# VectorE in source order from the first attention tile on, and ScalarE's part of a weight chunk one step sooner

## The chip, the core and the metric

The kernel runs on one core of a Trainium2 chip. A core has five engines with queues of their own: TensorE (matrix products, PE in the profile), VectorE (DVE), ScalarE (ACT), GpSimd (POOL) and SyncE (SP, which here only issues DMAs). They run side by side and wait for each other through semaphores; inside one queue everything happens in the order in which it stands there. The metric is the device time of one execution in microseconds (us).

## The reference

Attention with a position bias, and a gated feed-forward block behind it, all in float32:

```python
scores = scale * q @ k.T + bias            # q, k, v: 4 batches x 8 heads x 576 x 64
bias   = relu(x @ w1 + b1) @ w2            # x = log1p(|i-j|) / log1p(max(i,1)); hidden 32
attn   = softmax(scores) @ v               # -> x: 2304 tokens x 512
out    = ((x @ w_a) * (x @ w_b)) @ w_out   # w_a, w_b: 512 x 1536; w_out: 1536 x 512
```

The weights come as 64-bit numbers and are turned into 32-bit floats on the core.

## The kernel before

**Attention tiles.** The work is cut into 144 tiles of 128 query rows by 576 keys. A unit is a pair of heads of a batch; units 0 to 15 (tiles 0 to 63) are the first 256 rows of all batches, the others the rest. The first 16 tiles take their scores two at a time (`qk_pair`), from then on `qk` fills one buffer, which the next tile needs empty. For one tile: `qk` on TensorE; `soft1` (L539: the softmax pass on VectorE, which adds the bias, scales and takes the row minimum `mn`; L544: the exponential on ScalarE, with the row sum `sm`); `soft2` (L589: GpSimd adds a small number to the sum; L590: VectorE's reciprocal; L595: GpSimd multiplies the tile by it); `turn` (L607: five transposes on TensorE, copied back by ScalarE); and per unit `pv` (L635), whose output is split into two halves of 16 bits by ScalarE (L648) and VectorE (L650, the remainder). From unit 12 on `split_turn` (L574, L577, a DMA transpose) takes the place of the multiplication and `turn`. `prep_k`, `prep_q` and `prep_v` split K, Q and V of the units from 8 on the same way: ScalarE makes the upper half (L419, L433, L460), VectorE the remainder (L416, L435, L461).

**Weights.** 24 chunks of w_a and w_b, then 12 of w_out. A chunk is loaded (`w_load`), and `w_unit` turns it: ScalarE multiplies the upper word (L266), VectorE shifts it (L268), puts in three bits of the lower word (L269) and the sign (L272). For w_a and w_b a step `s` of `wab_steps` holds the conversion of chunk s, ScalarE's maximum over chunk s-1 (L289), every fourth step a power-of-two scale that goes through TensorE twice (`pow2_down`, L79 to L87, and `pow2_up`, L92, L94), and the split of chunk s-7 (`wab_parts`: L306 GpSimd, L309 ScalarE, L310 GpSimd). The tile `wt` that a chunk fills comes from two rings of four and is free again after L310, so chunk s needs the tile of chunk s-8. For w_out the split is L313 and L314 in the same step.

**MoE.** `moe_main` runs in blocks of 256 tokens: per 128 of the 1536 columns two half-steps of 12 matmuls (L768), ScalarE's scaled copy `asb` (L776) and VectorE's product `g` (L752, the gate); then `moe_out` (L812).

**What sets the order.** `merge` lays the generators side by side in source order: attention half-steps (`asteps`, two per tile), MoE half-steps (`main`) and weight steps (`wts`). Weight steps lie between tiles 0 and 46; the first MoE block begins at tile 19. TensorE issues in source order throughout (`manual_schedule`). VectorE does so only from the middle of the second MoE block on, which is tile 46 (`SOON`); ahead of it, and for ScalarE, GpSimd and SyncE throughout, a planner with a timing model picks the order. Around `SOON` the order in the source changes: below it a tile's `soft1` stands in its first half-step and `soft2` of the tile before at the end; from it on `soft2(n)` is followed by `soft1(n+1)`, and the remainders of K, Q and V (`lows`) are put off until after that.

## Time and profile before

| | us |
|---|---|
| median of 3 runs (lowest to highest) | 756.22 (755.72 to 757.78) |
| the profiled execution | 754.13 |
| its span, first to last instruction | 752.3 |
| TensorE busy | 699.4 (93%) |
| VectorE busy | 497.0 (66%) |
| ScalarE busy | 449.1 (60%) |
| GpSimd busy | 333.1 (44%) |
| mean granted TensorE clock | 0.984 |

The profiled execution is one run; its own time is a little under the median of the three. The busy shares are means over stages with different loads. A matmul's end is modelled, so a busy TensorE need not be at its peak.

### The profile page before, as it was taken

The numbers are of one execution on the slowest core, as the hardware profiler recorded it, in microseconds if no ns is written. First come the engines' busy times: TensorE is split into PE (matmuls) and PEld (weight loads), VectorE is DVE, ScalarE is ACT, GpSimd is POOL, SyncE is SP. The second block draws the span as 40 slices with busy tenths as digits, with TensorE's granted clock in tenths as the row PEclk, the third lists the DMA queues.
The fourth block names the chain that finished last, engine by engine and source line by source line (L and its number), as shares of the span: only waits on it lengthen the run. The fifth ranks groups of instructions, "written<-read, shape, count | busy, mean of one in ns | idle before, by whom it ended". The sixth has DMA issues, their size and how long they took to land.

```text
span 752.3 us, 15601 instructions
## 1 busy us (share of the span) xinstructions
PE 699.4 (93%) x5451; PEld 533.1 (71%) x5451; DVE 497.0 (66%) x1204; ACT 449.1 (60%) x1005; POOL 333.1 (44%) x477
## 2 busy tenths in 40 slices
PE   7787898899899999998899989999999999999997
PEld 2255465577787556676787768878888887888886
DVE  7768688858984576766798888888987781111100
ACT  6868887877876678754555556656655562321310
POOL 3437668865863123332354445634553562311200
PEclk9979999999999999999999999999999999999999
DMA  8998776477754887799999999999999974000001
GB/s 247 322 370 279 241 224 212 147 256 251 248 149 119 219 200 195 187 201 204 246 251 253 225 274 244 248 228 276 246 236 271 222 142 130 1 1 29 2 15 42
DMA packets 178163, 147.69 MB, mean 196 GB/s; under 512 B 125092, under 2 KB 138148, under 8 KB 178084
## 3 DMA queue, kind: packets, MB, share of 16 engines
q1 hardware_dynamic: 170928, 130.92, 69.4%
q10 hardware_dynamic: 5876, 10.93, 5.3%
q0 software_dynamic: 1280, 4.84, 1.8%
q8 instruction: 43, 0.70, 0.4%
q14 instruction: 36, 0.29, 0.1%
HBM read 101.15 MB, written 17.18 MB: 157 GB/s over the span
## 4 chain that ended last, share of the span: by engine, by line
PE 57%; DVE 11%; issue 9%; ACT 9%; POOL 7%; DMA 6%; SPq 0%; ACTq 0%; POOLq 0%; DVEq 0%
PE ab L768 25%; PE o L812 14%; PE pv L635 5%; PE qk L511 4%; DMA pt<-ph 3%; PE psta L155 3%; POOL ph L574 2%; DMA bias<-bias_d 2%; DVE p L539 2%; ACT p L544 2%; PE pr L888 2%; DVE wt L272 2%; PE tp L607 2%; DVE w16t L269 1%; POOL gl L788 1%
## 5 line engine op out<-in xcount | busy, mean ns | idle before, releaser
L768 PEld LDWEIGHTS <-w16t 128*128 128x128 f16 x2592 | 247.1, 98 | 47.1 <-issue 15.8
L768 PE MATMUL ab<-x,w16t 128*128 128x256 f16 x2304 | 270.4, 273 | 3.6 <-DVE x L650 3.3
L544 ACT ACTIVATE p<-p,mn 128x576 f32<-128x576 f32 x144 | 111.6, 775 | 72.9 <-DVE mn L539 63.1
L539 DVE CUSTOM_DVE_ANT_0 p<-qk,bias 128x576 f32<-128x576 f32 x144 | 107.3, 746 | 27.7 <-PE qk L511 11.5
L577 DVE SCALAR_TENSOR_TENSOR ph<-p,sm,ph 128x64 f16<-128x64 f32 x192 | 109.0, 608 | 20.6 <-POOL ph L574 20.0
L574 POOL TENSOR_SCALAR ph<-p,sm 128x576 f16<-128x576 f32 x96 | 71.5, 745 | 115.0 <-DVE sm L590 102.5
L812 PE MATMUL o<-wos,gh 128*128 128x512 f32 x384 | 120.3, 394 | 0.0
L788 POOL TENSOR_TENSOR gl<-g,gh 128x256 fp32r<-128x256 f32 x96 | 73.2, 762 | 89.9 <-ACT gh L787 89.9
L589 POOL TENSOR_SCALAR sm<-sm 128x1 f32<-128x1 f32 x144 | 59.0, 410 | 104.1 <-ACT p L544 99.8
L752 DVE SCALAR_TENSOR_TENSOR g<-ab,wv,asb 128x256 f32<-128x256 f32 x84 | 40.3, 480 | 81.9 <-ACT asb L776 80.7
L787 ACT CAST gh<-g 128x256 fp32r<-128x256 f32 x96 | 38.8, 404 | 75.8 <-DVE g L752 75.7
L812 PEld LDWEIGHTS o<-wos,gh 128*128 128x128 f32 x384 | 69.5, 188 | 16.0 <-issue 3.7
L511 PE MATMUL qk<-ks,qs 128*128 128x288 f32 x384 | 73.6, 313 | 6.0 <-DVE mn L539 4.2
L812 PE MATMUL o<-wos,gl 128*128 128x512 f32 x192 | 75.0, 391 | 0.0
L511 PEld LDWEIGHTS qk<-ks,qs 128*128 128x128 f32 x384 | 56.4, 190 | 16.1 <-DVE mn L539 5.8
L776 ACT ACTIVATE asb<-ab,wv 128x256 f32<-128x256 f32 x84 | 39.4, 469 | 29.0 <-PE ab L768 26.9
L595 POOL TENSOR_SCALAR p<-p,sm 128x576 f32<-128x576 f32 x48 | 43.9, 914 | 26.8 <-DVE sm L590 21.9
L635 PE MATMUL pv<-pt,vs 128*64 128x320 f16 (+1 forms) x560 | 43.5, 310 | 8.6 <-DMA pt<-ph 8.6
L635 PEld LDWEIGHTS <-vs 128*64 128x64 f16 x560 | 32.3, 115 | 21.3 <-issue 9.8
L607 PE MATMUL tp<-idn,p 128*128 128x128 f32 x240 | 38.3, 294 | 5.6 <-ACT ptf L612 4.1
L416 DVE TENSOR_TENSOR ks<-rk,ks 64x576 fp32r<-64x576 f32 x48 | 39.6, 824 | 3.7 <-ACT ks L419 2.2
L818 ACT COPY osb<-o 128x512 f32<-128x512 f32 x18 | 10.5, 583 | 52.2 <-PE o L812 36.4
(102 smaller groups left out, 964.2 us busy)
## 6 DMA issues: line engine op xcount, KB each, us to landing
bias<-bias_d SPq DMA_DIRECT2D x128, 288.0 KB, 3.9
rv<-vd SPq DMA_DIRECT2D x32, 320.0 KB, 4.5
rk<-kd SPq DMA_DIRECT2D x24, 288.0 KB, 3.3
wraw<-wa SPq DMA_DIRECT2D x12, 512.0 KB, 7.4
wraw<-wb SPq DMA_DIRECT2D x12, 512.0 KB, 5.7
wraw<-wo SPq DMA_DIRECT2D x12, 512.0 KB, 4.5
bias_d<-bo ACTq DMA_DIRECT2D x20, 295.5 KB, 3.7
bias_d<-bo POOLq DMA_DIRECT2D x16, 295.5 KB, 6.5
```

The source lines that it names most:

```text
L511: nc.tensor.matmul(ps[:, hf, :HB], a, b[:, hf * HB:hf * HB + HB], start=(x == 0), stop=(x == len(prods) - 1))
L539: ttr = nc.vector.tensor_tensor_reduce(out=p.rearrange("p (a n) -> p a n", a=2), in0=ps[:, :, :HB], in1=bt.rearrange("p (a n) -> p a n", a=2),
L544: exps.append(nc.scalar.activation(p, p, AF.Exp, bias=mn, scale=-1.0, accum_out=sm))
L574: nc.gpsimd.tensor_scalar(out=ph[:, :S], in0=p, scalar1=rc, scalar2=1.0, op0=ALU.mult, op1=ALU.mult)
L577: ins = nc.vector.scalar_tensor_tensor(out=ph[:, o:o + c1 - c0], in0=p[:, c0:c1], scalar=rc, in1=ph[:, c0:c1], op0=ALU.mult, op1=ALU.subtract,
L589: nc.gpsimd.tensor_scalar(out=sm, in0=sm, scalar1=1e-9, scalar2=1.0 / (PS if u >= NF else 1.0), op0=ALU.add, op1=ALU.mult)
L595: nc.gpsimd.tensor_scalar(out=p, in0=p, scalar1=rc, scalar2=1.0, op0=ALU.mult, op1=ALU.mult)
L607: nc.tensor.transpose(tp[:, x, :], p[:, c0:c0 + 128], tab["idn"])
L635: nc.tensor.matmul(ps[64 * j:64 * j + 64, o:o + N], v[:, j, :], p[:, j * N:j * N + N], start=(x == 0), stop=(x == len(prods) - 1),)
L768: nc.tensor.matmul(ab[:, j], w16[nm, f][:, pw, kk, :], xs[px][:, kk, :], start=(x % (3 * KC) == 0), stop=(x % (3 * KC) == 3 * KC - 1),)
L788: nc.gpsimd.tensor_tensor(out=gl, in0=g, in1=gh.bitcast(F32), op=ALU.subtract)
L812: nc.tensor.matmul(o, g[:, sl], wos[f][:, p], start=(f == 0 and x == 0), stop=(f == FC - 1 and x == 2))
```

## The change

VectorE's `manual_schedule` begins at the first attention tile. The order that held from tile 46 on (turn, qk, `soft2(n)`, `soft1(n+1)`, then remainders, then `pv`) holds for all tiles, and the remainders always wait in `lows`. `w_unit` is cut in two: `w_first` is ScalarE's multiplication, which now writes into the chunk's final place (w_a, w_b) or into the one tile that is used (w_out) and is emitted one step sooner; the rest stays with its step and takes the sign from the raw chunk. Inside a weight step the conversion and the loads come first, ahead of the scale and the split.

```diff
-    def w_unit(wt, raw, u=None):
-        lo, hi = raw[:, :, 0], raw[:, :, 1]
-        t = wt.tile([128, 512], I32, tag="wt", name="wt", bufs=4)
-        nc.scalar.mul(t.bitcast(F32), hi.bitcast(F32), REBIAS)
-        u, s = (t, hi) if u is None else (u, t)
-        nc.vector.tensor_scalar(out=u, in0=t, scalar1=3, scalar2=None, op0=ALU.logical_shift_left)
+    def w_first(raw, u):
+        nc.scalar.mul(u.bitcast(F32), raw[:, :, 1].bitcast(F32), REBIAS)
+        return u
+
+    def w_unit(raw, u, t):
+        lo, s = raw[:, :, 0], raw[:, :, 1]
+        nc.vector.tensor_scalar(out=u, in0=u, scalar1=3, scalar2=None, op0=ALU.logical_shift_left)
...
         fetch_to(3)
+        firsts = {0: wab_first(0, raws[0][1])}
         yield
         for s in range(4 * np_ + 7):
             p, c = divmod(s - 7, 4)
+            if s < 4 * np_:
+                pool, raw = raws.pop(s)
+                wfs[s] = wab_conv(pool, raw, firsts.pop(s))
+                pool = raw = None
+                fetch_to(s + 1 + min(6, 3 + s // 2))
+                if s + 1 < 4 * np_:
+                    firsts[s + 1] = wab_first(s + 1, raws[s + 1][1])
...
-            if s < 4 * np_:
-                wfs[s] = wab_conv(s, *raws.pop(s))
-                fetch_to(s + 1 + min(6, 3 + s // 2))
...
+        t = first(0)
         yield
         for f in range(FC):
             with late():
-                wf = w_unit(wt, raws[f], wt.tile([128, 512], I32, tag="wt", name="wu", bufs=4))
+                wf = w_unit(raws[f], t, t)
                 wo_split(f, wf)
...
+            if f + 1 < FC:
+                t = first(f + 1)
...
-        if not lows[0]:
-            lows_now()
...
-            if n <= SOON:
+            if n == 0:
                 soft1(n)
...
-            if SOON <= n < 3 * N0 + 2:
+            if 2 <= n < 3 * N0 + 2:
                 turn(n - 2, tpp)
...
-            if SOON <= n <= NT:
-                if n == SOON:
-                    run(soft2(n - 1))
+            if n <= NT:
                 s2 = soft2(n) if n < NT else iter(())
                 next(s2, None)
                 if n + 1 < NT:
...
-            if 2 <= n < SOON:
-                turn(n - 2, tpp)
...
-            if 1 <= n < SOON:
-                run(soft2(n - 1))
             yield
...
+        ctx.enter_context(tc.manual_schedule(engines={mybir.EngineType.DVE}))
         keep(8)
         merge((asteps, 4), (wts, 1), ((keep(2) for _ in range(4)), 4))
...
-        ctx.enter_context(tc.manual_schedule(engines={mybir.EngineType.DVE}))
         merge((main, 2 * FC - 22 + GS + 1), (asteps, n2 - n2 * 5 // 8))
```

## Rows read from the trace of the kernel before

**Rows 1.** Windows: start:end, length, busy us (x instructions) by engine, granted clock, DMA

```profile
36.47:94.88 58.41, 49.60 (x358) 30.26 (x358) 42.01 (x117) 46.19 (x109) 34.49 (x51) 0.91 0.85 296
94.88:142.45 47.57, 42.45 (x330) 29.43 (x329) 40.59 (x100) 39.26 (x88) 35.30 (x43) 1.00 0.66 208
142.45:175.03 32.58, 29.17 (x227) 21.96 (x225) 21.68 (x54) 24.46 (x52) 21.66 (x29) 0.95 0.69 225
175.03:227.76 52.73, 49.93 (x418) 42.20 (x416) 45.84 (x91) 42.94 (x92) 36.21 (x40) 0.97 0.67 210
440.00:617.00 177.00, 175.10 (x1500) 146.46 (x1499) 150.31 (x350) 105.62 (x244) 89.20 (x135) 1.00 1.11 239
```

**Rows 2.** Waits: engine line <- releaser: us in total, times, longest

```profile
PE qk L502 <- DVE mn L539: 5.1, 3, 2.5
PE qk L511 <- DVE mn L539: 4.2, 4, 2.6
...
DVE w16t L268 <- ACT wt L266: 5.0, 6, 1.7
...
DVE w16t L268 <- ACT wt L266: 1.8, 2, 1.0
...
DVE sm L590 <- POOL sm L589: 13.4, 15, 2.1
```

**Rows 3.** Timeline, 143 to 150: start, length, instruction, [idle before <- releaser]

```profile
143.64 0.76 PE L502 MATMUL qk<-rkf,rqf 64*128 64x288 f32 x4
...
144.99 2.40 DVE L416 TENSOR_TENSOR ks<-rk,ks 64x576 fp32r<-64x576 f32 x2 [1.71 <-ACT ks L419]
...
149.27 1.17 PE L502 MATMUL qk<-rkf,rqf 64*128 64x288 f32 x4 [2.46 <-DVE mn L539]
```

**Rows 4.** Timeline, 190 to 198, VectorE and TensorE

```profile
190.06 1.65 DVE L272 SCALAR_TENSOR_TENSOR wt<-wt,wu 128x512 int32<-128x512 int32 x1
...
196.39 0.74 DVE L539 CUSTOM_DVE_ANT_0 p<-qk,bias 128x576 f32<-128x576 f32 x1
...
190.70 0.77 PE L511 MATMUL qk<-ks,qs 128*128 128x288 f32 x4
...
197.20 1.29 PE L511 MATMUL qk<-ks,qs 128*128 128x288 f32 x4 [2.57 <-DVE mn L539]
```

**Rows 5.** Groups by line: instruction xcount | busy us, mean ns | idle before

```profile
L269 DVE SCALAR_TENSOR_TENSOR w16t<-wraw,w16t 128x512 int32<-128x512 int32 x24 | 20.0, 832 | 0.3
L272 DVE SCALAR_TENSOR_TENSOR wt<-wt,w16t 128x512 int32<-128x512 int32 x24 | 19.2, 802 | 0.1
L268 DVE TENSOR_SCALAR w16t<-wt 128x512 int32<-128x512 int32 x24 | 12.8, 534 | 6.8 <-ACT wt L266 6.8
```

**Rows 6.** Timeline, 108 to 115: one ring tile from chunk to chunk

```profile
108.89 1.16 POOL L310 TENSOR_TENSOR w16t<-wt,w16t 128x512 f16<-128x512 f32 x1
...
110.14 0.68 ACT L266 ACTIVATE wt<-wraw 128x512 f32<-128x512 f32 x1
...
113.89 1.23 DVE L272 SCALAR_TENSOR_TENSOR wt<-wt,w16t 128x512 int32<-128x512 int32 x1
```

**Rows 7.** Timeline, 160.9 to 163.2: one tile's loop

```profile
160.98 0.76 DVE L539 CUSTOM_DVE_ANT_0 p<-qk,bias 128x576 f32<-128x576 f32 x1 [0.22 <-PE tp L607]
...
161.83 0.78 ACT L544 ACTIVATE p<-p,mn 128x576 f32<-128x576 f32 x1
...
163.01 0.16 DVE L590 RECIPROCAL sm<-sm 128x1 f32<-128x1 f32 x1
```

**Rows 8.** By line: xcount, shortest/median/longest ns, first and last start us

```profile
L539 DVE CUSTOM_DVE_ANT_0 p<-qk,bias x144: 729/745/759, 36.5 to 617.3; 128x576 f32<-128x576 f32 x144
...
L268 DVE TENSOR_SCALAR wu<-wt x12: 407/426/1516, 169.4 to 220.0; 128x512 int32<-128x512 int32 x12
...
L269 DVE SCALAR_TENSOR_TENSOR wu<-wraw,wu x12: 675/776/1639, 169.9 to 220.7; 128x512 int32<-128x512 int32 x12
...
L272 DVE SCALAR_TENSOR_TENSOR wt<-wt,wu x12: 669/904/1654, 170.8 to 222.2; 128x512 int32<-128x512 int32 x12
```

**Rows 9.** Timeline, 155: the remainder of a PV product

```profile
155.35 0.48 DVE L650 SCALAR_TENSOR_TENSOR x<-pv,vs,x 128x256 f16<-128x256 f32 x1 [2.60 <-ACT x L648]
```

More of the change, by code (lines that the diff above doesn't have):

```diff
@@ L50 @@
 VS = N0 - 4, 2 * N0 - 4, 3 * N0 - 10
-SOON = 3 * N0 - 2
 @with_exitstack
@@ L278, in attention_moe, with wab_first, wab_conv @@
     w16t = cst.tile([128, FC, 2, 2, KC, 128], F16, name="w16t")
-    def wab_conv(n, wt, raw):
+    def wab_first(n, raw):
         with late():
-            return w_unit(wt, raw, w16t[:, n // 2, n % 2].rearrange("p x k n -> p (x k n)").bitcast(I32))
+            return w_first(raw, w16t[:, n // 2, n % 2].rearrange("p x k n -> p (x k n)").bitcast(I32))
+    def wab_conv(wt, raw, u):
+        with late():
+            return w_unit(raw, u, wt.tile([128, 512], I32, tag="wt", name="wt", bufs=4))
     def wab_size(f, j, wf, m):
@@ L351, in wab_steps, with first @@
                 wab_size(2 * p + c // 2, c % 2, wfs[s - 1], ms[p])
-            if s < 4 * np_:
-                wfs[s] = wab_conv(s, *raws.pop(s))
-                fetch_to(s + 1 + min(6, 3 + s // 2))
             yield
     def wo_steps(wt):
+        def first(f):
+            with late():
+                return w_first(raws[f], wt.tile([128, 512], I32, tag="wt", name="wu", bufs=4))
         raws = [w_load(wt, wo, f) for f in range(2)]
+        t = first(0)
         yield
@@ L361, in wo_steps @@
             with late():
-                wf = w_unit(wt, raws[f], wt.tile([128, 512], I32, tag="wt", name="wu", bufs=4))
+                wf = w_unit(raws[f], t, t)
                 wo_split(f, wf)
-            raws[f] = None
+            raws[f] = t = wf = None
             if f + 2 < FC:
                 raws.append(w_load(wt, wo, f + 2))
+            if f + 1 < FC:
+                t = first(f + 1)
             yield
     st = {}
-    lows = [False, []]
+    lows = []
     def lows_now(k=9):
-        for _ in range(min(k, len(lows[1]))):
-            lows[1].pop(0)()
+        for _ in range(min(k, len(lows))):
+            lows.pop(0)()
     def load_unit(u):
@@ L419, in prep_k @@
             nc.scalar.copy(ks[sl, j], rk[sl])
-            lows[1].append(partial(low, j))
-        if not lows[0]:
-            lows_now()
+            lows.append(partial(low, j))
         st["ks", u] = ks
@@ L433, in prep_q @@
         nc.scalar.copy(d[:, 0], s)
-        lows[1].append(
+        lows.append(
             lambda: nc.vector.tensor_tensor(out=d[:, 1], in0=s, in1=d[:, 0].bitcast(F32), op=ALU.subtract)
         )
-        if not lows[0]:
-            lows_now()
         st["qs", u] = dst
@@ L460, in prep_v @@
         nc.scalar.mul(hi, rv, vsc[UNITS[u][0]][0])
-        lows[1].append(lambda: nc.vector.scalar_tensor_tensor(
+        lows.append(lambda: nc.vector.scalar_tensor_tensor(
             out=lo, in0=rv, scalar=vsc[UNITS[u][0]][0], in1=hi, op0=ALU.mult, op1=ALU.subtract
         ))
-        if not lows[0]:
-            lows_now()
         st["vs", u] = vs
@@ L684, in attn_steps @@
                 elif ahead == 3:
-                    lows[0] = n >= SOON
                     with late():
@@ L694, in attn_steps @@
                         v_tail()
-                    lows[0] = n >= SOON
                     with late():
```

## The prediction, made before the changed kernel had run

> **What bounds the kernel now.** I read the table of windows first, cut at the places where the work changes, because the page's shares average over stages with different limits. Tiles 0 to 18 run from 36.47 to 94.88 us (stage A), tiles 19 to 28 to 142.45 (stage B), tiles 29 to 45 to 227.76 (stage C, two rows); from tile 46 on, VectorE is already in source order and the change alters nothing [rows 1]. The reader is to see that TensorE is idle for 58.41 - 49.60 = 8.8 us in A, 5.1 us in B and 3.4 + 2.8 = 6.2 us in C, and that from 440 us on, with VectorE in source order and 150.3/177 = 85% busy, TensorE is busy 99% of the time. VectorE is 85% and 87% busy in B and the second part of C: there two nearly full engines lose time to each other. In A TensorE is no limit: no MoE block runs yet and part of its work only fills time; there the limit is the loop of one tile through four engines, with ScalarE 79% busy.
>
> Then the waits. TensorE waits 5.1 us in 3 and 4.2 us in 4 pieces, before a score matmul (qk), for the softmax pass of the tile before (mn), which must empty the one qk buffer of these tiles; VectorE waits 5.0 us in A and 1.8 us in B for ScalarE's first pass over a weight chunk, and 13.4 us in 15 pieces for the sum that the reciprocal needs [rows 2]. Last, the timeline around the two longest TensorE waits shows what VectorE did instead. At 144.99 it has waited 1.71 us for ScalarE and then splits two halves of K (2.40 us) and after them Q, all ahead of the softmax pass; qk starts at 149.27, 2.46 us late, and takes 1.17 us where it took 0.76 at 143.64 [rows 3]. At 190.06 it is busy with weight chunks; the pass whose scores were ready at 191.5 (190.70 + 0.77) starts at 196.39, the next qk is 2.57 us late and takes 1.29 instead of 0.77 us [rows 4]. So the order in which VectorE takes its work, not its amount, holds TensorE there.
>
> **The change, part by part.**
>
> *K, Q and V remainders no longer ahead of the softmax pass (stage C).* In the new order the pass of tile n+1 stands right behind the reciprocal of tile n, and the remainders behind it. That takes away the first pattern: 2.46 us, and with it the small waits among the 4.2 us of L511 that have the same cause. *Weight chunks in their source place.* At most about 11 chunks fall on 10 tiles while w_out is converted, so between two softmax passes stands one chunk or two, not the two to three of 190 to 196 us; the second pattern shrinks or goes: 2.57 of the 4.2 us. With both waits goes what followed them: the granted clock is 0.95 over 32.58 us and 0.97 over 52.73 us [rows 1], so 1.6 us of TensorE's full-speed work is lost in each; after both waits the matmuls ran at the 1.2 GHz level, as their durations show [rows 3, 4]. All of C's part together: 2.46 + 4.2 + 1.6 + 1.6 = 9.9 us. What is late next is the pass behind one chunk (0.53 + 0.83 + 0.80 = 2.17 us [rows 5]) and a gate; TensorE has two to three half-blocks of matmuls to cover it, not always. I take two thirds: -6.5 us, ends -9.9 and 0 (the waits come back elsewhere).
>
> *ScalarE's pass one step sooner.* It was emitted just before VectorE's three operations that need it; now a step ahead. It removes up to 6.8 us of VectorE waiting, 5.0 in A and 1.8 in B. Added instructions: none; the result is written into the chunk's final place, and the scratch tile is claimed only by the last of the three operations. The old ScalarE pass had to wait for the tile to come free: GpSimd ends with the chunk eight earlier at 110.05, ScalarE starts at 110.14, and VectorE's last operation at 113.89 [rows 6]. Now that last operation alone waits, and 3.7 us of chain shorten to one operation. The cost: if GpSimd is late, VectorE itself stands, with the next reciprocal and pass queued behind. For w_out the new form uses one tile instead of two and reads the sign from the raw chunk; L269 reads the raw chunk in the same way, 0.83 against 0.80 us [rows 5], so I cost this at 36 x 0.03 = 1 us of VectorE at most, inside its idle time, and nothing below. DMA: the raw tile is free one operation later (0.8 us), and SyncE's loads behind it with it; loads run three to six chunks ahead, so nothing.
>
> *Reciprocal before the next softmax pass (stage A).* The old code emitted the pass first and the reciprocal later, and left the choice to the planner. Now every tile is a loop: pass at 160.98, exponential from 161.83, GpSimd's sum, reciprocal at 163.01, and the next pass can follow 0.08 later: 2.11 us [rows 7], of which VectorE is free for 1.35. Nineteen tiles are 40 us. A chunk in the gap takes 1.75 us (the shortest of its three operations, 0.407 + 0.675 + 0.669 [rows 8]) to 2.17 us (the means), so 0.4 to 0.8 us over the gap, times 11 chunks: 4 to 9 us. The other VectorE work (42.0 - 19 x 0.92 - 11 x 1.75 = 5.3 us) partly falls in gaps without a chunk. That is 44 to 54 us against 58.4 now, on undisturbed waits; ScalarE alone needs 46.2 and the DMA engines are 85% busy [rows 1], so most of the difference will not be had. I take -2, ends -7 and +4 (the free 1.35 us of a loop lost once more in three tiles, where ScalarE or GpSimd has something ahead).
>
> *Stage B.* VectorE's work is 40.6 of 47.6 us. The waits for ScalarE go (1.8); TensorE's waits before qk (5.1 - 2.46 = 2.6 us) get shorter by what piled-up chunks cost; new waits come (below). I take -1, ends -5 (TensorE never idle) and +5.
>
> TensorE's order changes too: the five transposes stand ahead of qk instead of behind. Both belong to older or ready tiles; zero, from -0.5 to +0.5. After 228 us everything moves with the front: from 440 us TensorE is full; before that the loads follow the tiles, and their order stays.
>
> Sum: -6.5 - 2 - 1 = -9.5 us. The profiled execution took 754.13, so 744.6; the median of the runs is 756.22, 2.1 above it, so 746.7, and I say 747.
>
> *A rule against the trace.* Softmax passes, with one input from TensorE's output memory, took 729 to 759 ns wherever they stood, while L272, which reads two tensors, took 669 to 1654 ns [rows 8]. The Trainium skill (SBUF — State Buffer, "Who interferes with whom") says that a VectorE instruction with two SBUF inputs and a GpSimd instruction that reads SBUF exclude each other, and that one with at most one SBUF input and outside the two-port modes does not. The durations fit it. By that rule the change decides who runs beside GpSimd, which is the rival "less contention" below.
>
> **The rivals.**
>
> 1. *Slower: VectorE stands in line (0.24).* The place is B and the second row of C. In source order, the remainder of a PV product stands right behind the softmax pass, and behind it the next chunk. It waits for 20 matmuls and a ScalarE copy: the one time the old order let that happen it cost 2.60 us [rows 9]. With one per four tiles, some 5 in these 100 us cost 13 us; the last operation of a chunk waiting for GpSimd at the first chunk of each group (4 groups, about 2 us) makes 8 more. VectorE's idle time there is 7.0 + 6.9 = 13.9 us [rows 1]; from the point where the new waits exceed that, TensorE is late. 21 - 13.9 = 7 us, with C's clock kept and half its waits gone -2, gives +5 on 754.13, which is 761 beside the median. For it: the two engines are both near full. Against it: from 440 us on the same order, PV remainder included, keeps TensorE at 99% beside a VectorE at 85%.
>
> 2. *No change (0.13).* The waits before qk go, but others (reciprocal behind the sum, pass behind qk) take their place at the same price; 755 to 757 us. For it: the waits for the sum are already VectorE's largest here [rows 2]. Against: TensorE's idle time in C has two named places which the new order cannot produce.
>
> 3. *Less contention (0.13).* The reciprocal starts GpSimd's normalization, and the next thing on VectorE is now a softmax pass, which does not suffer from it; before, it was often a chunk. If the 11 chunks of B fall from 2.17 to 1.75 us, and the 12 of w_out from the medians' 0.426 + 0.776 + 0.904 = 2.11 to 1.75 [rows 5, 8], VectorE gains 4.6 + 4.3 = 9 us in B and C. Half of that, 4.5 us, is what TensorE's idle time there still holds beyond the forecast; with A at its better end, 5 more: 737 us. Against it: GpSimd's longest operations (splits of weights) are not moved away from the chunks.
>
> **How the numbers follow.** Forecast 0.50, rivals 0.24, 0.13 and 0.13. The forecast's own range is 741 to 756 (each term half-way to its end, added). For eight in ten I go from 735, below rival 3, to 761, the middle of rival 1. About 0.3%, 2.3 us, is what can be told from no change. Faster: 0.13 from rival 3, nearly all of the forecast, a little of rival 2: 0.63. Same: 0.13. Slower: 0.24.
>
> **What would show it.** Right: TensorE's waits before qk for mn fall below 3 us between 95 and 228 us; granted clock 1.00 in C; VectorE's wait for ScalarE's pass over a chunk gone; tile 46 starts before 221 us. Step by step: A's 19 tiles in 55 to 58 us, C in under 80 instead of 85.3. Wrong: waits of the PV remainder or of the chunk's last operation (for GpSimd) above 14 us in total, with TensorE idle behind them; or A longer than 60 us, which would mean that the loop, not the engines' work, was its limit.

## The result: 1.5% slower, and the profile after

The changed kernel took 767.16 us (median of 4 runs, 766.43 to 770.62) against 756.24 for the kernel before, a ratio of 1.015 [1.0116, 1.0184]. The forecast was 747, its range ended at 761. The profiled execution took 767.5, with a span of 765.7 and a mean clock of 0.979 (before: 752.3 and 0.984).

First stage C in its two rows, cut at the same tiles as in [rows 1] (columns as there):

```profile
155.81:186.21 30.40, 28.05 (x234) 21.76 (x233) 19.14 (x54) 24.40 (x52) 20.35 (x27) 1.00 0.71 229
186.21:239.33 53.12, 45.70 (x372) 37.60 (x370) 44.94 (x89) 40.49 (x86) 35.36 (x41) 0.94 0.65 210
```

By this cut C is 1.8 us shorter (30.40 + 53.12 against 32.58 + 52.73), and that is a trap: its second row holds 372 matmuls where before it held 418. The softmax passes, which mark the cut, now run further ahead of TensorE's queue: tile 46's pass stands 7.4 us ahead of the first output matmul, where it stood 4.0 ahead. A fair cut goes by TensorE itself, which issues in source order in both kernels: from tile 0's pass to the first MoE matmul (A), from there to the PV product at 151.63 us before and 162.55 after (B), and from there to the first output matmul (C). Before, then after:

```profile
36.47:95.52 59.05, 50.24 (x362) 30.56 (x361) 42.64 (x118) 46.82 (x110) 35.13 (x52) 0.91 0.85 295
95.52:151.63 56.11, 48.53 (x369) 33.51 (x368) 46.66 (x113) 46.30 (x103) 42.65 (x52) 0.98 0.63 198
151.63:231.75 80.12, 75.91 (x625) 61.72 (x624) 62.54 (x134) 62.58 (x132) 52.53 (x63) 0.97 0.70 222
```
```profile
37.72:101.48 63.76, 51.07 (x361) 30.75 (x360) 40.21 (x115) 47.59 (x110) 29.81 (x49) 0.92 0.78 269
101.48:162.55 61.07, 50.38 (x370) 34.37 (x369) 48.74 (x113) 44.40 (x99) 40.05 (x51) 0.94 0.57 176
162.55:246.70 84.15, 75.64 (x626) 61.08 (x624) 64.80 (x138) 64.10 (x136) 54.03 (x67) 0.96 0.68 219
```

The matmul counts now agree within one. The loss is +4.7 us in A, +5.0 in B and +4.0 in C, after a start that was 1.25 later: 14.95 us at the first output matmul, of which the span keeps 13.4. TensorE's idle time grew from 8.8 to 12.7, from 7.6 to 10.7 and from 4.2 to 8.5 us; and its matmuls take longer in B (50.4 against 48.5, at a clock of 0.94) and a little in A (51.1 against 50.2).

From here on line numbers are the changed kernel's: the pass is L549, qk is L512 or L521, the reciprocal L600, the transposes are L617, the remainder of a PV product is L574 (first 16 tiles) or L660. What TensorE waited for, from 102 to 240 us (engine, line, releaser: total us, times, longest), and under it VectorE's waits from 37.72 to 239.33:

```profile
PE qk L512 <- DVE mn L549: 6.1, 4, 2.6
PE pr L78 <- DVE vm L229: 5.5, 2, 4.4
PE tp L617 <- ACT ptw L627: 4.2, 4, 1.5
PE pr L78 <- ACT w16t L293: 3.0, 2, 1.7
PE qk L521 <- DVE mn L549: 0.3, 1, 0.3
```
```profile
DVE sm L600 <- POOL sm L599: 14.9, 11, 2.7
DVE x L660 <- ACT x L658: 7.0, 5, 2.9
DVE x L574 <- ACT x L573: 6.5, 5, 2.9
DVE wt L272 <- POOL w16t L314: 5.2, 3, 1.7
```

Against [rows 2]: the wait for ScalarE's pass over a chunk is gone, and in C the wait of qk for the pass fell from 4.2 to 0.3 us, as forecast. In B it did not fall: 6.1 us in 4 pieces (L512), where the same stage of the kernel before has 5.1 in 3. So the two together are 6.4 us, and the sign of being right was "below 3". Of its other signs three more failed: tile 46 starts at 239.33 us and not before 221, C takes 83.5 us by the tiles and not under 80, and its clock is 0.96 and not 1.00. New are the PV remainder (L574 in A, 6.5 us in 5 pieces, and L660 in B and C, 7.0 in 5), the chunk's last operation behind GpSimd (L272, 5.2 us, one of the three pieces in A), and on TensorE a line that the forecast had not named: L78, the matmul that turns the maximum over V, 4.4 us in one piece.

Three stretches of the timeline after show how work that TensorE waits for stands behind long work. At the end of A, VectorE and TensorE:

```profile
86.18 0.38 PE L91 MATMUL pr<-p2d,one 4*128 4x4 f32 x2
...
86.34 0.42 DVE L268 TENSOR_SCALAR w16t<-w16t 128x512 int32<-128x512 int32 x1
86.79 0.69 DVE L269 SCALAR_TENSOR_TENSOR w16t<-wraw,w16t 128x512 int32<-128x512 int32 x1
...
87.52 0.69 DVE L272 SCALAR_TENSOR_TENSOR wt<-wraw,w16t 128x512 int32<-128x512 int32 x1
88.13 0.15 DVE L93 COPY p2g<-pr 128x4 f32<-128x4 f32 x1
...
88.34 1.01 PE L890 MATMUL pr<-w16t 128*128 128x512 f16 x2 [1.78 <-DVE p2g L93]
...
89.14 1.27 PE L617 MATMUL tp<-idn,p 128*128 128x128 f32 x5
...
90.35 1.26 PE L512 MATMUL qk<-rkf,rqf 64*128 64x288 f32 x4
...
91.65 0.76 DVE L549 CUSTOM_DVE_ANT_0 p<-qk,bias 128x576 f32<-128x576 f32 x1 [2.98 <-PE qk L512]
```

The scale's copy L93 (0.15 us) is ready at 86.56 and stands behind a whole chunk until 88.13, because the change put the conversion first in the weight step. A matmul that only keeps TensorE busy (L890) waits for it 1.78 us; then transposes and qk run at the 1.2 GHz level (1.27 and 1.26 where 0.71 and 0.76 are usual; the granted clock from 88.34 to 91.61 is 0.53), and the next pass is 2.98 us late. VectorE shows no wait at L93: it was busy. In B, VectorE and TensorE at the second chunk of a pair:

```profile
118.44 1.63 DVE L272 SCALAR_TENSOR_TENSOR wt<-wraw,w16t 128x512 int32<-128x512 int32 x1 [1.72 <-POOL w16t L314]
120.00 0.15 DVE L600 RECIPROCAL sm<-sm 128x1 f32<-128x1 f32 x1
120.07 0.73 DVE L549 CUSTOM_DVE_ANT_0 p<-qk,bias 128x576 f32<-128x576 f32 x1
...
120.86 0.76 PE L512 MATMUL qk<-rkf,rqf 64*128 64x288 f32 x4 [2.60 <-DVE mn L549]
```

Here VectorE itself stands, 1.72 us for GpSimd, with the reciprocal and the pass behind it, and qk is 2.60 us late. The same happens again at 136.17 and 138.98 (1.72 and 2.63): these two make 5.2 of B's 6.1 us. And near the end of C, where TensorE's L78 waits for a reduction of 0.14 us:

```profile
223.43 0.42 DVE L268 TENSOR_SCALAR wu<-wu 128x512 int32<-128x512 int32 x1
223.88 1.03 DVE L269 SCALAR_TENSOR_TENSOR wu<-wraw,wu 128x512 int32<-128x512 int32 x1
224.94 1.10 DVE L272 SCALAR_TENSOR_TENSOR wu<-wraw,wu 128x512 int32<-128x512 int32 x1
225.97 0.14 DVE L229 TENSOR_REDUCE vm<-vmx 128x1 f32<-128x4 f32 x1
...
226.17 0.59 PE L78 MATMUL pr<-idn,vm 128*1 128x128 f32 x2 [4.44 <-DVE vm L229]
226.69 2.74 PE L770 MATMUL ab<-x,w16t 128*128 128x256 f16 x12
```

What the reduction reads was complete at 219.23. Of the 4.44 us the chunk is 2.5; in the rest VectorE is busy with what stands ahead of the chunk, down from a remainder of Q.

### The profile page after: what moved, and what is told of

Its sections match the earlier page's. It is cut to its first block, busy times and chain, and to the rows that moved or that the text cites. A ratio compares the mean times of both kernels' runs of the same rounds, so it can differ in the third digit from the quotient of the medians.

```text
span 765.7 us, 15604 instructions
## 1 busy us (share of the span) xinstructions
PE 702.1 (92%) x5451; PEld 533.7 (70%) x5451; DVE 499.5 (65%) x1204; ACT 450.4 (59%) x1005; POOL 325.4 (43%) x477
## 4 chain that ended last, share of the span: by engine, by line
PE 55%; DVE 10%; issue 10%; POOL 10%; ACT 8%; DMA 6%; SPq 1%; ACTq 0%; POOLq 0%; DVEq 0%
PE ab L770 25%; PE o L814 14%; PE pv L645 5%; PE qk L521 4%; POOL ph L584 3%; ACT p L554 2%; PE psta L154 2%; POOL sm L599 2%; DMA pt<-ph 2%; PE tp L617 2%; DVE p L549 2%; POOL w16t L314 1%; POOL gl L790 1%; POOL wt L310 1%; DMA bias_d<-bo 1%
## 5 line engine op out<-in xcount | busy, mean ns | idle before, releaser
L770 PE MATMUL ab<-x,w16t 128*128 128x256 f16 x2304 | 274.0, 276 | 3.3 <-DVE x L660 3.3
L549 DVE CUSTOM_DVE_ANT_0 p<-qk,bias 128x576 f32<-128x576 f32 x144 | 107.1, 743 | 28.5 <-PE qk L521 14.3
L790 POOL TENSOR_TENSOR gl<-g,gh 128x256 fp32r<-128x256 f32 x96 | 75.0, 782 | 92.4 <-ACT gh L789 92.3
L521 PE MATMUL qk<-ks,qs 128*128 128x288 f32 x384 | 73.5, 313 | 2.7 <-DVE qs L449 1.8
L521 PEld LDWEIGHTS qk<-ks,qs 128*128 128x128 f32 x384 | 56.6, 190 | 11.7 <-issue 5.4
L605 POOL TENSOR_SCALAR p<-p,sm 128x576 f32<-128x576 f32 x48 | 36.9, 769 | 37.6 <-DVE sm L600 33.4
L617 PE MATMUL tp<-idn,p 128*128 128x128 f32 x240 | 36.9, 287 | 10.5 <-ACT ptw L627 4.2
L617 PEld LDWEIGHTS tp<-idn,p 128*128 128x128 f32 x240 | 28.8, 148 | 18.4 <-issue 8.1
L814 PEld LDWEIGHTS o<-wos,gl 128*128 128x128 f32 x192 | 36.0, 188 | 7.8
```

The source lines that it names most:

```text
L521: nc.tensor.matmul(ps[:, hf, :HB], a, b[:, hf * HB:hf * HB + HB], start=(x == 0), stop=(x == len(prods) - 1))
L549: ttr = nc.vector.tensor_tensor_reduce(out=p.rearrange("p (a n) -> p a n", a=2), in0=ps[:, :, :HB], in1=bt.rearrange("p (a n) -> p a n", a=2),
L617: nc.tensor.transpose(tp[:, x, :], p[:, c0:c0 + 128], tab["idn"])
L770: nc.tensor.matmul(ab[:, j], w16[nm, f][:, pw, kk, :], xs[px][:, kk, :], start=(x % (3 * KC) == 0), stop=(x % (3 * KC) == 3 * KC - 1),)
L790: nc.gpsimd.tensor_tensor(out=gl, in0=g, in1=gh.bitcast(F32), op=ALU.subtract)
L814: nc.tensor.matmul(o, g[:, sl], wos[f][:, p], start=(f == 0 and x == 0), stop=(f == FC - 1 and x == 2))
```

## The experiments

All times of stages below are A, B and C by TensorE's marks, each from one profiled execution; the ratio to the kernel before is from the repeated runs. How far one execution strays can be read from those that have a stage unchanged: B took 60.96 to 61.07 us (after, e9, e6, e7, e16), A 62.3 to 63.8 (after, e9, e16), C 82.2 to 84.3 (after, e9, e5, e7). From the first output matmul to the end all runs took 516 to 523 us, so a few microseconds won by then need not be seen at the end of one execution.

| kernel | A | B | C | ratio [95%] |
|---|---|---|---|---|
| before | 59.05 | 56.11 | 80.12 | 1 |
| after | 63.76 | 61.07 | 84.15 | 1.015 [1.0116, 1.0184] |
| e9 (after, again) | 62.31 | 60.96 | 84.26 | 1.0132 [1.0086, 1.0178] |
| e1 | 57.79 | 55.72 | 82.79 | 1.0007 [0.9971, 1.0042] |
| e2 | 56.65 | 55.08 | 78.18 | 0.9998 [0.9968, 1.0028] |
| e3 | 57.69 | 58.32 | 83.34 | 1.0103 [1.0069, 1.0138] |
| e4 | 56.18 | 56.21 | 84.40 | 1.0034 [1.0002, 1.0067] |
| e5 | 65.02 | 59.79 | 82.18 | 1.0187 [1.0149, 1.0225] |
| e6 | 67.47 | 61.03 | 79.57 | 1.0162 [1.0120, 1.0204] |
| e7 | 62.11 | 61.05 | 83.10 | 1.0175 [1.0137, 1.0213] |
| e8 | 63.62 | 60.31 | 81.74 | 1.0135 [1.0091, 1.0179] |
| e10 | 61.02 | 58.48 | 83.13 | 1.0106 [1.0068, 1.0145] |
| e11 | 59.78 | 58.55 | 83.96 | 1.0088 [1.0059, 1.0117] |
| e12 | 61.96 | 56.69 | 79.04 | 1.0044 [1.0011, 1.0077] |
| e13 | 62.46 | 54.77 | 80.30 | 1.0019 [0.9994, 1.0044] |
| e14 | 57.07 | 56.89 | 80.26 | 0.9988 [0.9960, 1.0017] |
| e15 | 59.85 | 55.81 | 79.85 | 0.9987 [0.9962, 1.0012] |
| e16 | 62.53 | 61.03 | 80.01 | 1.0121 [1.0088, 1.0153] |
| e17 | 59.49 | 56.69 | 80.26 | 1.0000 [0.9978, 1.0022] |
| e18 | 57.26 | 54.76 | 80.31 | 0.9968 [0.9943, 0.9993] |

**Which part of the change costs: e1 to e4.** e1 is the kernel before with the weight code alone (`w_first`, conversion first in its step), VectorE planned as before. e2, e3 and e4 are the changed kernel with one line moved: VectorE's source order begins at tile 46, at tile 19, or at about tile 32.

```diff
-        ctx.enter_context(tc.manual_schedule(engines={mybir.EngineType.DVE}))
         keep(8)
...
+    ctx.enter_context(tc.manual_schedule(engines={mybir.EngineType.DVE}))   # e3
     main, (_, n1) = moe_main(0, 0, mps), steps(1)
...
+    ctx.enter_context(tc.manual_schedule(engines={mybir.EngineType.DVE}))   # e4
     merge((main, 2 * FC - 19), (asteps, n1 - n1 * 4 // 5), (wts, 3))
...
+        ctx.enter_context(tc.manual_schedule(engines={mybir.EngineType.DVE}))   # e2
         merge((main, 2 * FC - 22 + GS + 1), (asteps, n2 - n2 * 5 // 8))
```

> Only ScalarE's pass one step sooner, with the three VectorE operations and the loads first in their step; VectorE planned and attention ordered as before. Theory (VectorE standing in line in stages A and B makes the loss): 754 to 758 us, since the planner still fills VectorE's gaps; its waits for ScalarE's pass (6.8 us) fall below 2 us and TensorE's waits before qk stay near 9 us. Rival (the earlier ScalarE pass and the later claim of the scratch tile make the loss): 762 us or more.

> The whole changed source, but VectorE in source order only from tile 46 on, as before; ahead of it the planner picks. Theory (standing in line): 752 to 759 us, as the planner may again let a chunk pass a waiting operation. Rival (the new source order of tiles itself, transposes ahead of qk and the reciprocal ahead of the next pass, makes the loss): 763 us or more, with the loss of stage A still there.

> The changed source, VectorE in source order from tile 19 on (stages B and C), planned in A. Theory: A gives back its 6.4 us, B keeps its 5.7 us: 759 to 762 us; the last operation of a chunk still waits about 1.7 us for GpSimd at the first chunk of each group. Rival (the loss of A is not VectorE's order): 765 to 768 us.

> The changed source, VectorE in source order from about tile 32 on, behind the chunks of w_a and w_b. Theory: A and B as before, the first part of C gains some 2 us, its second part still pays TensorE's wait for the maximum over V (4.4 us): 752 to 757 us. Rival (any start in source order before tile 46 costs, since both engines are full): 760 us or more.

e1 and e2 cannot be told from the kernel before: neither the weight code nor the new tile order costs anything that these runs can show while the planner orders VectorE. The loss is the source order, and it adds up by where it begins: 0.3% from tile 32, 0.7% more from 19, 0.3 to 0.5% more from 0 (e9 and the first comparison). In the table A rises in neither e3 nor e4; B rises by 2.2 us in e3, and by the full 5 only with source order from the first tile, so these shares are not those of the stages one by one. C is 83 to 84 us in e3 and e4, but the planned C strays too (78.18 in e2, 82.79 in e1), so C's share needs e6.

e2 also tells what the waits that the forecast went for were worth. From the first MoE matmul to the first output matmul TensorE waits 1.4 us for the pass (mn) in it, against 9.3 in the kernel before and 11.8 in e1, and the times of the three cannot be told apart. Other waits stand in their place: 4.5 us for ScalarE's copies of the transposes, and 4.2 us for its maxima over weight chunks (before: none, and 2.5). TensorE's waits in e2 from 93.92 to 227.18:

```profile
PE tp L617 <- ACT ptw L627: 4.5, 4, 2.6
...
PE qk L521 <- DVE mn L549: 1.4, 1, 1.4
```

**Single waits taken away: e5 to e8.** Each is the changed kernel with one edit. e6's acts on the second, third and fourth batch element (its text below names the second only): the maximum keeps its place, and the matmul that turns it comes a step later. The wait at 226 us belongs to the fourth.

```diff
-            p, c = divmod(s - 7, 4)                                # e5
+            p, c = divmod(s - 6, 4)
...
-                    wab_parts(p, c, wfs.pop(s - 7), rms[p])
+                    wab_parts(p, c, wfs.pop(s - 6), rms[p])
...
+        if b:                                                      # e6
+            yield
         dg = pow2_down(m1, 1, "v")
         yield
-        if b:
-            yield
...
+            if n < N0:                                             # e7
+                soft1(n + 1)
+                run(soft2(n))
+                lows_now(2)
-            if n <= NT:
+            elif n <= NT:
...
-        nc.vector.scalar_tensor_tensor(                            # e8
+        xlows.append(lambda: nc.vector.scalar_tensor_tensor(
...
                 lows_now(2)
+                xlows_now()
```

> Base: the changed kernel, VectorE in source order from the first tile. One edit: a chunk of the first two weights is split on GpSimd one step sooner (six steps behind its conversion instead of seven), so the ring tile that VectorE's last chunk operation needs comes free a step sooner. Nothing is left out. Theory (VectorE stands in line in B behind L272's wait for GpSimd's split, 5.2 us in 3 pieces of 1.7, each followed by a late softmax pass and a slower clock): the three waits fall below 0.5 us each, and stage B shortens by 3 to 6 us: ratio to the kernel before about 1.009 instead of 1.015. Rival (the waits only show that VectorE is early; the next thing in line, the sum for the reciprocal, ends last anyway): the waits go, L600's wait for the sum grows by as much, and the time stays at 1.013 to 1.017.

The three waits are gone from the list, but B is only 1.2 to 1.3 us shorter instead of 3 to 6, and the ratio, 1.0187, is no lower: the rival was right that the time stays, though not in where it goes. The sum's wait did not grow (10.7 us in all, against 14.9). The waits of qk for the pass went as well, 6.1 us in B. In their place TensorE waits 7.2 us in B for ScalarE's maxima over the chunks (L293; 3.0 in the changed kernel) and 3.3 us around the scale's second matmul (L91; 0 in the changed kernel): with the split a step sooner, the scale's second matmul comes one step behind its first and not two. The longest of these waits:

```profile
137.07 0.38 PE L78 MATMUL pr<-idn,wm 128*4 128x128 f32 x2 [3.84 <-ACT w16t L293]
```

The chunks themselves became slower too, 30.1 us of VectorE in B against 27.9. VectorE's two chunks between two passes, and GpSimd beside them:

```profile
113.21 0.63 DVE L268 TENSOR_SCALAR w16t<-w16t 128x512 int32<-128x512 int32 x1
113.88 1.05 DVE L269 SCALAR_TENSOR_TENSOR w16t<-wraw,w16t 128x512 int32<-128x512 int32 x1
114.96 1.06 DVE L272 SCALAR_TENSOR_TENSOR wt<-wraw,w16t 128x512 int32<-128x512 int32 x1
115.95 1.37 DVE L268 TENSOR_SCALAR w16t<-w16t 128x512 int32<-128x512 int32 x1
117.36 0.69 DVE L269 SCALAR_TENSOR_TENSOR w16t<-wraw,w16t 128x512 int32<-128x512 int32 x1
118.15 1.46 DVE L272 SCALAR_TENSOR_TENSOR wt<-wraw,w16t 128x512 int32<-128x512 int32 x1
```
```profile
113.53 1.96 POOL L310 TENSOR_SCALAR wt<-wt,rm 128x512 f32<-128x512 f32 x2
115.46 1.58 POOL L314 TENSOR_TENSOR w16t<-wt,w16t 128x512 f16<-128x512 f32 x1
...
117.45 1.61 POOL L314 TENSOR_TENSOR w16t<-wt,w16t 128x512 f16<-128x512 f32 x1
```

Six operations take 6.3 us where the chunk at 86.34 took 1.8, so two would take 3.6. Even so the pass, at 119.61, comes 15.7 us after the first MoE matmul, and the same pass of the changed kernel, at 120.07, 18.6: the edit gains 2.9 us up to here, and more than half of that is lost again by the end of B.

> Base: the changed kernel. One edit: for the second batch element, VectorE's maximum over V is emitted one step ahead of the matmul that turns it, instead of just before it. Nothing is left out. Theory (TensorE, in order too, stands 4.4 us at 226 us behind a matmul whose input is queued on VectorE behind two weight chunks): the wait falls below 1 us, the slow-clock stretch behind it goes, and the tiles from 46 on come 3 to 6 us sooner: ratio 1.007 to 1.011. Rival (TensorE catches up by 440 us or the transfers of later units set the pace): the wait goes, but less than 1.5 us of it is left at the end: 1.013 to 1.016.

The place is mended: L78 waits 0.70 us for the maximum, and C takes 79.57 us, 4.6 less than in both executions of the changed kernel. Over all runs with C in source order (in e4 and e15 from tile 32), the nine without this edit took 81.7 to 84.4 us, the eight with it 79.0 to 80.3.

```profile
228.14 0.14 DVE L229 TENSOR_REDUCE vm<-vmx 128x1 f32<-128x4 f32 x1
...
228.34 0.38 PE L78 MATMUL pr<-idn,vm 128*1 128x128 f32 x2 [0.70 <-DVE vm L229]
```

The ratio does not show it, since A took 67.47 us. I first put that down to stray; it was the edit. The second batch element's maximum falls into the end of A, and there the matmul that turns it now comes one step later, so that L80, the reduction behind it, stands behind a PV remainder, which waits for ScalarE, and a chunk. VectorE and TensorE in e6:

```profile
95.83 0.38 PE L78 MATMUL pr<-idn,vm 128*1 128x128 f32 x2
...
97.37 0.35 DVE L574 SCALAR_TENSOR_TENSOR x<-pv,vs,x 128x128 f16<-128x128 f32 x1 [2.87 <-ACT x L573]
...
98.81 0.69 DVE L272 SCALAR_TENSOR_TENSOR wt<-wraw,w16t 128x512 int32<-128x512 int32 x1
99.42 0.27 DVE L80 TENSOR_REDUCE p2m<-pr 1x1 f32<-1x128 f32 x1
...
99.75 1.01 PE L890 MATMUL pr<-w16t 128*128 128x512 f16 x2 [3.54 <-DVE p2m L80]
```

Short work behind long work again, 3.54 us of TensorE's time at another place, but here VectorE's own wait has a part in it: e16 tests it.

> Base: the changed kernel. One edit: in the first 19 tiles the softmax pass of tile n+1 stands ahead of the reciprocal of tile n, as in the source of the kernel before; VectorE stays in source order. Nothing is left out. Theory A (stage A is 6.4 us longer because the next pass stands behind the reciprocal, which waits for exponential and sum: a loop through four engines for each tile): VectorE's wait for the sum in A falls by half, and stage A ends 3 to 6 us sooner, ratio 1.008 to 1.012. Theory B (the loop is no limit; what costs in A is the remainder of a PV product and the turned maximum standing behind other work): A changes by less than 1.5 us, ratio 1.013 to 1.017.

VectorE's wait for the sum fell by half (8.0 us), but A is 62.11 us, no shorter than e9's 62.31: theory B, though the ratio, 1.0175, is a little above its range. The reciprocal ahead of the pass, on which the forecast for A rested, is no limit either way.

> Base: the changed kernel. One edit: the remainder of a PV product on VectorE (it waits for 20 matmuls and ScalarE's copy) stands behind the next softmax pass instead of right where the product is issued, but for the last pair of heads and the last units. Nothing is left out. Theory (rival 1 of the prediction: VectorE stands 6.5 us in A for it and 7.0 us in B and C, with the next chunk and pass queued behind): these 13.5 us of waits fall below 4, and the time by 3 to 7 us: ratio 1.006 to 1.011. Rival (the wait falls where VectorE has room; what stands next in line ends as late): waits move to the sum for the reciprocal or to the qk matmul, and the ratio stays at 1.012 to 1.017.

The waits of the PV remainder fall from 13.5 to 2.6 us, one piece of L574 in A. A stays (63.62), B is 0.7 and C 2.4 us shorter; VectorE's waits for qk (L512) grow from 4.2 to 7.0 and for `asb` from 3.0 to 5.7 us. C's part is not clear of stray: among the runs with e6's edit, C took 79.6 to 80.0 us without this one (e6, e15, e16) and 79.0 to 80.3 with it (e12, e13, e14, e17, e18). So the waits were worth 0.7 us in B and at most about 3 in all, and the ratio, 1.0135, lies in the rival's range and cannot be told from the changed kernel's.

**The chunk as a block: e9 to e12.** e9 is the changed kernel once more. e10 puts the conversion last in its step, e11 puts a chunk's last operation behind the next softmax pass, e12 is e10, e6 and e8 together.

```diff
                 wab_size(2 * p + c // 2, c % 2, wfs[s - 1], ms[p])
+            if s < 4 * np_:                                        # e10: moved here from
+                pool, raw = raws.pop(s)                            # the head of the step
+                wfs[s] = wab_conv(pool, raw, firsts.pop(s))
...
-        last.append(nc.vector.scalar_tensor_tensor(                # e11
+        tails.append(lambda: last.append(nc.vector.scalar_tensor_tensor(
...
                     soft1(n + 1)
+                tails_now()
                 run(s2)
```

> The changed kernel once more, beside the three that follow, since the four before it moved the time by less than chips and stage A differ from one execution to the next. Every theory expects 1.012 to 1.018, and says by its stages how far one execution strays: first MoE matmul at 99 to 105 us, first output matmul at 243 to 247 us.

It came out so: 1.0132, with the first MoE matmul at 99.25 and the first output matmul at 244.47 us.

> Base: the changed kernel. One edit: within a step of the first two weights, the conversion of a chunk stands last again, as in the kernel before, so the short VectorE operations of the step (the copy of the turned maximum, which TensorE waits for, its reciprocal and the reductions) stand ahead of the chunk and not behind it. Nothing is left out. Theory (a chunk in source order is a block of 1.8 to 2.2 us, and TensorE, in order too, stands behind the short operation that is queued behind it, then runs at the lower clock): the 2.0 us wait of TensorE for the copy at the end of A goes, tiles 16 to 19 take 12 to 14 us instead of 16.9, the first MoE matmul comes 3 to 6 us sooner; ratio 1.007 to 1.012. Rival (the copy now stands at the head and waits for TensorE itself, with chunk and pass behind it, so the wait only changes its name): tiles 16 to 19 stay at 16 to 17 us, ratio 1.013 to 1.018.

The same stretch as at 86.18 in the changed kernel, in e10:

```profile
85.57 0.38 PE L91 MATMUL pr<-p2d,one 4*128 4x4 f32 x2
...
85.98 0.16 DVE L93 COPY p2g<-pr 128x4 f32<-128x4 f32 x1 [0.17 <-PE pr L91]
...
86.20 0.59 PE L890 MATMUL pr<-w16t 128*128 128x512 f16 x2 [0.25 <-DVE p2g L93]
...
86.63 0.71 PE L617 MATMUL tp<-idn,p 128*128 128x128 f32 x5
...
87.27 0.76 PE L512 MATMUL qk<-rkf,rqf 64*128 64x288 f32 x4
```

TensorE waits 0.25 us instead of 1.78 and keeps its clock (granted 1.00 from 86.20 to 88.00); VectorE pays 0.17. A is 1.3 to 2.7 us shorter than in the two executions of the changed kernel (which lie 1.5 apart) and B 2.5 us; the ratio is in the theory's range, though its interval overlaps the changed kernel's. The theory was too high in A: the first MoE matmul came 0.6 and 2.8 us sooner than in those two, not 3 to 6, and tiles 16 to 19 took 14.7 us, where the two took 15.5 and 16.9. In B the edit is not only about short operations: VectorE's waits of L272 fell from 5.2 to 1.0 us with it, and qk's for the pass from 6.1 to 1.7.

> Base: the changed kernel. One edit: the last of a chunk's three VectorE operations stands behind the next softmax pass instead of right behind the second, so the reciprocal and the pass wait for two operations (1.1 us) and not three (1.8). Nothing is left out. Theory (the chunk is too long a block for the gap between exponential and reciprocal): VectorE's reciprocal and pass come 0.7 us sooner in each tile with a chunk, A and B shorten by 3 to 6 us together: ratio 1.007 to 1.012. Rival (the gap of 1.35 us per tile covers a chunk nearly; what costs is the few places where TensorE waits for a short operation): less than 2 us, 1.012 to 1.017.

Against the two executions of the changed kernel A is 2.5 and 4.0 us shorter and B 2.5, and the ratio is at the theory's place: the length of the block counts. The wait for GpSimd moved behind the pass together with the operation (4.4 us in 2 pieces), so in B the two are not told apart.

> Base: the changed kernel, with three edits together: a chunk's conversion last in its step, the maximum over V a step ahead of the matmul that turns it, and the remainder of a PV product behind the next softmax pass. Nothing is left out. Theory (the three are separate places where short work stands behind long work; the gains add: 3 to 6 us in A, 3.8 at the end of C as the single edit showed, 2 to 3 for the remainder): 756 to 759 us, ratio 1.000 to 1.005. Rival (what is taken away in one place is late in the next, as in three of the four single edits): ratio 1.009 to 1.014. If it comes out under 0.997, the source order was the better choice after all, and only its order within the steps was wrong.

The gains add: 759.49 us. B is back at 56.7 and C at 79.0 us; A is not (61.96).

**Where the rest is: e13 to e15.** e13 adds e11's edit to e12. e14 is e12 with the source order from tile 19 on (e3's line), e15 is e4 with e6's edit.

> Base: the changed kernel with the three edits of e12 (chunk last in its step, maximum over V a step sooner, PV remainder behind the next pass), and a fourth: the chunk's last operation behind the next softmax pass. Nothing is left out. Theory (what is left of the loss, 0.4%, is the chunk as a block in A and B; the split alone was worth 0.4%): ratio 0.998 to 1.002. Rival (the split and the chunk in last place take away the same waits, so they don't add): 1.003 to 1.007.

> The planner orders VectorE up to tile 18, source order from tile 19, with the three edits of e12. Nothing is left out. Theory (A's share of the loss is 0.5%, and most of it is left with the three edits, since first MoE matmul still comes 3 to 5 us later than in the planned order): 0.998 to 1.002, some 3 us faster than the three edits in source order from the first tile. Rival (the edits have mended A as well, and where the source order starts no longer matters): 1.003 to 1.006.

> The planner orders VectorE up to about tile 32, source order from there, with one edit: the maximum over V a step sooner. Nothing is left out. Theory (in C the source order takes 3 to 4 us from TensorE's waits before qk, as forecast, and gave them back in one place, 4.4 us of waiting for the turned maximum and a slow clock behind it; with that place mended, C's gain stays): first output matmul 229 to 231 us where the same order without the edit had 234.0; ratio 0.996 to 1.000. Rival (the planner's own order of C is as good): 1.001 to 1.004.

e13 is at the theory's upper end; B is 54.77 us, A still 62.46. e14 gives A back to the planner: 57.07 us, 755.17 against e12's 759.49, so the rest sits in A. e15 takes 4.55 us from e4's C by setting one reduction a step ahead of its matmul, and the loss of 0.3% goes with it; its first output matmul came at 232.63 and not at 229 to 231 because A took 59.85 us and not e4's 56.18. Both hold 1 in their intervals.

**A's rest: e16 to e18.** e16 is e6 without its part in A; e17 is e13, and e18 is e13 with e3's line, both with that same correction.

```diff
-        if b:                                                      # e16, against e6
+        if b > 1:
             yield
         dg = pow2_down(m1, 1, "v")
         yield
+        if b == 1:
+            yield
```

> Base: the changed kernel. One edit: e6's, but for the third and fourth batch element only; the second's maximum, which falls into the end of A, stays as the change left it. Nothing is left out. Theory (e6's edit moved the matmul that turns the maximum one step later in A too, and there the reduction behind it, L80, came to stand behind a chunk, with TensorE waiting 3.5 us: the gain of 4.6 us in C was taken back by the same mechanism in A, and A's 67.5 us was not stray): A 61 to 64 us, C 79 to 81, first output matmul 239 to 242, ratio 1.007 to 1.011. Rival (A's length was stray of one execution): A anywhere from 62 to 68, ratio 1.012 to 1.018 like e6's.

> Base: e13, source order from the first tile with four edits, but the maximum over V is moved for the third and fourth batch element only. Nothing is left out. Theory (the 2.5 us of TensorE waiting for L80 at 96 us in e12 is what is left in A): A 58 to 60.5 us instead of 62.5, ratio 0.996 to 1.001. Rival (A's rest is spread over its tiles): A 61 to 63, 1.000 to 1.004.

> e17's edits, with the planner ordering VectorE up to tile 18 (e3's line). Nothing is left out. Theory (A planned at 56 to 60 us; B 54 to 56 and C 79 to 81 in source order with the edits): ratio 0.994 to 0.999, the best of these versions. Rival (the planner's B and C are as good, and nothing below the kernel before is to be had from VectorE's order): 0.998 to 1.001.

e16 settles e6: A is 62.53 us, the wait for L80 is down to 0.4, C keeps its 80.01, and the first output matmul is at 240.47. The ratio ends at 1.0121, a little above the theory's range and at the foot of the rival's; its interval reaches into both. A's length would fit both as well, so it is the wait, gone with the edit's part in A, that decides. In e17 A comes to 59.49 us and the time to that of the kernel before: source order from the first tile, with its short operations mended, costs nothing any more that can be told. Against e13 only A is shorter. B took 56.69 us and not 54.77, with TensorE idle as long (6.8 and 6.6 us) but at a clock of 0.94 instead of 0.97, and the two ratios cannot be told apart. e18 is the one version that beats both kernels, 751.92 us, though by 0.3% only, which is the bound of what can be told.

## Why the prediction was wrong, step by step

**The bound before** was read rightly from the lines, but not in what it was worth. The wait for ScalarE's pass went, and so did qk's waits in C; those in B did not (5.1 us before, 6.1 after). And where the planner takes nearly all of them away (e2, 1.4 us left), the time stays that of the kernel before: other waits stand in their place.

**Stage C, forecast -6.5, measured +4.0.** C's waits of qk for the pass did go (4.2 to 0.3 us). What failed is "the waits come back elsewhere", which was priced at 0 at worst: they came back as 4.4 us behind the maximum over V and 2.7 us behind ScalarE's copies of the transposes. With the first of these mended C is 79.85 us (e15), inside what the planned C took (78.2 to 82.8): no gain, no loss. Even then the forecast gain is not there. "One chunk or two between two softmax passes" was right and looked harmless; I had asked only what the pass waits for, not which other VectorE operations TensorE waits for. The price of 9.9 us was too high as well: it counts 6.7 us of waits in windows in which TensorE is idle for 6.2.

**ScalarE's pass one step sooner: 6.8 us of waiting removed, worth nothing that can be told (e1).** This is the step that failed most plainly as a reading of the diff: it prices ScalarE's pass and the tile, and leaves out that the conversion moved to the head of the step, past `pow2_up` and its copy to TensorE. Under a planner the place in the source is nothing (e1); in source order it cost what e10 gives back, 2.5 us in B and up to 2.7 in A.

**Stage A, forecast -2, worst +4, measured +4.7.** The loop of pass, exponential, sum and reciprocal was the wrong limit (e7). The eight executions with a planned A took 56.2 to 59.9 us; in the change's own order (after, e9, e16) A took 62.3 to 63.8, and with the short operations ahead and the chunk cut (e17) 59.5. The sign "A longer than 60 us" came true, its reading, "the loop was its limit", did not. (In the loop of 2.11 us VectorE is free for 1.27 and not 1.35, since the reciprocal takes 0.08 of it; nothing hangs on that.)

**Stage B, forecast -1, worst +5, measured +5.0**: at its bad end. Qk's waits were to get shorter and grew by 1.0 us; 5.2 of their 6.1 stand behind L272's wait for GpSimd, as rival 1 had it.

**Rival 1** named the right mechanism there, with the wrong sizes and the wrong rule. In its place, B and C, 13 + 8 us were priced and 7.0 + 3.4 were seen: less than the 13.9 us of idle time from which it was to decide, so that by its rule nothing would have been late. The 18.7 us in all are above its sign of 14 only because A counts. Nor were the waits the price: with the PV remainder's taken away 0.7 us of B come back, or a little more in C (e8), with L272's 1.2 to 1.3 (e5, beside the waits that its edit made). VectorE's idle time decides nothing in a queue: at L93 and L229 the cost lies where VectorE is *busy* with a chunk and an operation of 0.15 us behind it has TensorE waiting, and that shows in no wait of VectorE.

**Rival 3** did not come: the chunks' operations took 27.9 us in B, where they had taken 25.9, and 29.1 in C, where they had taken 29.7.

**What stays open.** A in e17 is still some 2 us over the middle of the planned executions; no single wait explains it. PV remainders and ring waits were taken away only whole, so how much of what came back is theirs and how much is a chunk that moved with them is not told apart. In B of e17, 5.1 of TensorE's 6.8 us of idle time are waits for ScalarE's maxima over the chunks (2.5 in the kernel before); no run took these away. The 1.5 us that came back between 247 us and the end were not followed up.

## What to carry to other kernels

Before an engine is put in source order, list its short operations that an in-order engine or the next loop step waits for, and look at what stands ahead of each in the source: a busy block costs there, and the engine's own waits need not show it. Put such operations ahead of long blocks or cut the blocks: four edits of the order took back the whole loss (e17), while taking away the waits that VectorE showed took back little by itself. And before a wait is priced, look for the one that stands behind it: where the qk waits went (e2), no time did. Compare stages by marks of the engine that keeps its order, with equal instruction counts, and look for an edit's own harm in the other stages before calling a difference stray.

## What was not expected of the hardware

A wait that goes can come back in part as slower instructions. In e5 the wait for GpSimd went, and the chunk's operations ran beside GpSimd's splits instead: L268 took 1.37 us beside L314 where it took 0.42 at 86.34 in the changed kernel, and L272 took 1.46 instead of 0.69. Over all of B that is 2.2 us of VectorE's time. The Trainium skill (SBUF — State Buffer, "Who interferes with whom") says that an instruction which holds the port pair that VectorE and GpSimd share keeps the other engine off that pair for its whole length; these durations agree with it, though no run here measured the port by itself. One short stall of TensorE costs more than its length: after the 1.78 us ahead of 88.34 the five transposes and four score matmuls took 2.53 instead of 1.47 us, at a granted clock of 0.53, and after the 4.44 us ahead of 226.17 twelve MoE matmuls took 2.74, at 0.50, where twelve such matmuls at 220.25 took 1.48 at 1.00.
